# Retention, gated MLP and SoLU on one core: eight half tiles of MLP weights converted one stage earlier, and raw weights loaded two ahead instead of three

## The chip, the core and the metric

One core of one Trainium2 chip runs the whole program. TensorE (PE) multiplies matrices, VectorE (DVE), ScalarE (ACT) and GpSimd (POOL) do the elementwise work, and SyncE (SP) issues every DMA of this kernel. Each engine takes its instructions strictly in the order of its own queue. The metric is the device time in microseconds; the median of three runs before is 684.48 us (682.38 to 685.29).

## The reference

Three layers follow one another over 2304 tokens of 512 features (4 sequences of 576 tokens, 8 heads of 64):

```
scores = scale * q @ k.T                      # per batch and head
x  = (scores * decay_mask) @ v                # decay gamma**(i-j), causal; 2304 x 512
h  = x @ w_in                                 # 512 -> 2048
g  = h * clip(h + 3, 0, 6) / 6
x2 = g @ w_out                                # 2048 -> 512
h2 = x2 @ w2_in                               # 512 -> 1024
solu = h2 * softmax(h2);  ln = layernorm(solu) * g_ln
out = ln @ w2_out                             # 1024 -> 512
```

The MLP weights arrive as 64-bit floats, taken as pairs of 32-bit words. The precision of a product is kept by splitting each operand into two parts (a rounded value and its remainder) and multiplying three of the four combinations, so one logical product is three matmuls.

## The kernel before, in words

**Tiles and stages.** Tokens are cut into five blocks, 0 to 3 of 512 tokens and 4 of 256 (`BLOCKS`). The 2048 hidden features are 16 tiles of 128 ("ff"). The first MLP runs in two parts: the first part takes ff 0 to 5 (`FIRST`) for all five blocks and stores partial sums `x2s` in DRAM; the second part takes ff 6 to 15 (`FB`), adds the stored partial sums and goes on to the second MLP. Attention comes first and is interleaved with block 0 of the first part; then come the end of block 0 beside the h products of block 1 (`mlp_turns`), the x2 products of block 1 (`mlp_x2s(1)`), then blocks 2, 3 and 4.

**One block of the first part** (`mlp`, L250): `mlp_h` (L202) makes, for each ff, 12 matmuls into one PSUM tile; ACT forms `r` from it (L219), DVE forms `gf` (L220), ACT rounds it to `g` (L223) and POOL takes the remainder (L224). `mlp_x2s` (L239) then makes, for each of four quarters `d` of the output, 18 matmuls over the six `g`, and `evac_partial` (L303) lets ACT copy the finished quarter out of PSUM (L305, tile `x2p`) and SP store it (L306). The PSUM tiles of h and of x2 share four buffers ("mm" in two pools of two), so a next h product waits until an earlier quarter has been copied out. The copies use two buffers (`x2e`), so the third copy of a block waits for the store of the first. Each generator yields after three matmuls; in blocks 1 to 3 a yield is three matmuls of 512 columns, 24 yields make the h phase and 24 the x2 phase. Block 4 runs `mlp_by_ff` (L269): h products alone for the first three ff, then h and x2 in turns.

**Conversion of weights** (class `Weights`, L89). Each ff has two halves (w_in and w_out). `load_to(n)` issues DMAs of raw halves (512 KB each, L102) up to number n; the raw tile `wraw` has two buffers (`WRAW`). `step()` loads ahead and converts the next half with `split` (L112): ACT L122, DVE L127, ACT L128, DVE L129, L130 (the last reader of the raw tile), L133, and L136 on DVE or, for every third half, on POOL. `ahead` says up to which half `step` has loads issued before it converts: with three, the load of the half two further on stands in the program before the conversion whose raw buffer it takes over; with two, the load of the next half stands there.

**Order.** The library orders the instructions of each queue when the program is built, from the data they need, the order in which the program traces them and its own planned times; the chip then keeps that order. `keep_in_program_order` fixes an instruction behind the one traced just before it on the same engine. All loads of raw weights (L101 to L103) are fixed in this way on SP, so that each stands behind whatever SP instruction was traced before it.

**Where the conversions stand before.** The 12 halves of ff 0 to 5 are converted during attention and `mlp_turns`. The eight halves of ff 6 to 9 (`FB[:4]`, tag `wb` of pool `pb`) are converted during block 3 of the first part, one at every sixth yield (L590 to L594). The 12 halves of ff 10 to 15 (`FB[4:]`, which take over the buffers of ff 0 to 5) are converted from the middle of block 4 on, through `first_b`, the first block of the second part, which itself begins to run inside the last yields of block 4 (L597 to L607). The 16 halves of the second MLP follow, one every 12 yields.

Of the kernel before, what the change touches and what calls it, by code (L numbers as in the profile page):

```python
# [22 lines left out]
NFF = DFF // 128  # L23
NFF2 = DFF2 // 128
FA = 6
# [12 lines left out]
A_FROM = 4  # L38
TAIL = 2
ACT_W = (1,)  # L40
AHEAD = 3
WRAW = 2
C_AHEAD = 8
EARLY = 3
# [13 lines left out]
def retention_hardswish_solu_kernel(ctx, tc, kt, qt, kn, vt, w1, w2i, w2o, gln, decay, place, out):  # L58
# [10 lines left out]
    def mm_tile(shape, name):  # L69
        turn[0] += 1  # L70
        return ps_mm[(turn[0] // 2) % len(ps_mm)].tile(shape, F32, tag="mm", name=name)
# [17 lines left out]
    class Weights:  # L89


        def __init__(self, halves, pin, ahead=AHEAD):
            self.pin, self.ahead = pin, ahead
            self.todo = list(halves)
            self.raws = []
            self.at = 0
# [47 lines left out]
    def w_half(home, i, name):  # L144

        if home == "w":
            return p0.tile([128, 2, 512], F32R, tag="wi" if i == 0 else "wo", bufs=FA, name=name)
        return pb.tile([128, 2, 512], F32R, tag="wb", bufs=8, name=name)

    def w1_halves(ffs, home, order):  # L150

        for k, i in order:
            ff = ffs[k]
            if (ff, 1 - i) not in w1t and home == "wb":
                for j in range(2):
                    w1t[ff, j] = w_half(home, j, f"w1_{ff}_{j}")

            def tile_of(ff=ff, i=i):
                if home == "w":
                    w1t[ff, i] = w_half(home, i, f"w1_{ff}_{i}")  # L160
                return w1t[ff, i]

            yield w1[ff][:, i * 1024:(i + 1) * 1024], tile_of

    def in_first(n):
        return [(k, i) for i in range(2) for k in range(n)]

    def in_turn(n, ahead):

        return sorted(in_first(n), key=lambda ki: (ki[0] + ahead * ki[1], -ki[1]))  # L170
# [56 lines left out]
    def mlp_x2(acc, ff, d, g, first, last):  # L227
        c = slice(d * 128, (d + 1) * 128)
        for i, (a, b) in enumerate(((0, 0), (1, 0), (0, 1))):
            nc.tensor.matmul(acc, w1t[ff, 1][:, a, c], g[:, b], start=(first and i == 0), stop=(last and i == 2))  # L230

    def mlp_hs(t, ffs, g, slot, keep_x=False):

        for k, ff in enumerate(ffs):
            if keep_x and 0 <= k - 1 < NP:
                tc.keep_in_program_order(nc.sync.dma_start(out=xs[t][:, k - 1], in_=f32(xb[t, k - 1])))
            yield from mlp_h(t, ff, g, slot)

    def mlp_x2s(t, ffs, g, evac):  # L239

        n = BLOCKS[t][1]
        for d in range(NP):
            acc = mm_tile([128, n], f"x2_{t}_{d}")
            for k, ff in enumerate(ffs):
                mlp_x2(acc, ff, d, g[ff], k == 0, k == len(ffs) - 1)
                if k == len(ffs) - 1:
                    evac(t, d, acc)
                yield

    def mlp(t, ffs, slot, evac, keep_x=False):  # L250
        g = {}
        yield from mlp_hs(t, ffs, g, slot, keep_x)
        yield from mlp_x2s(t, ffs, g, evac)

    def mlp_turns(t, g, hs, ffs, evac, ps):

        n = BLOCKS[t][1]
        accs = [ps.tile([128, 2, 512], F32, tag="h2", bufs=2, name=f"acc{t}_{i}") for i in range(2)]
        for k, ff in enumerate(ffs):
            for d in range(NP):  # L260
                mlp_x2(accs[d // 2][:, d % 2], ff, d, g[ff], k == 0, k == len(ffs) - 1)
                if k == len(ffs) - 1:
                    evac(t, d, accs[d // 2][:, d % 2])
            yield k
            for d in range(NP):
                next(hs)
            yield k

    def mlp_by_ff(t, ffs, slot, evac, ps, then=iter(()), n_then=0, ahead=0):  # L269


        n = BLOCKS[t][1]
        share = 512 // n
        accs = [
            ps.tile([128, 2, 512], F32, tag="h2", bufs=2, name=f"acc{t}_{ffs[0]}_{i}").rearrange(
                "p a (b n) -> p (a b) n", n=n
            ) for i in range(2 // share)
        ]
        g, done = {}, []
        last = len(ffs) - 1  # L280
        for k in range(len(ffs) + X2_LAG):
            h = mlp_h(t, ffs[k], g, slot) if k <= last else iter(())
            j = k - X2_LAG
            for d in range(NP):
                next(h, None)
                if 0 <= (k - last - 1) * NP + d + ahead < n_then:
                    next(then, None)
                if j >= 0:

                    acc = accs[d * n // 1024][:, d % (1024 // n)]  # L290
                    mlp_x2(
                        acc, ffs[j], d, g[ffs[j]],
                        j == 0 and d % share == 0, j == last and d % share == share - 1,
                    )
                    if j == last:
                        done.append((d, acc))
                        if (d + 1) * n % 1024 == 0:
                            for item in done:
                                evac(t, *item)
                            done.clear()  # L300
                yield j
# [152 lines left out]
    def attention():  # L454

        for pr in range(NPAIR + 1):
            if pr < NPAIR:
                scores(pr)
                yield pr
                if pr + 2 >= EARLY:  # L460
                    load_pair(pr + 2)
                chunk_states(pr)
                if pr == 0:
                    places()
                prep(pr + 1)
                if pr < NP:
                    widen(pr)
            if pr:
                values(pr - 1)
            yield pr  # L470
            if pr < NPAIR:
                last_scores(pr)
            if pr:
                from_states(pr - 1)
            yield pr
            if pr == 1:
                tc.keep_in_program_order(nc.sync.dma_start(out=gln_sb, in_=gln))
# [21 lines left out]
        )  # L499
    prep(0)  # L500

    FIRST = list(range(FA))
    g_a = lambda ff: (p0, "g", FA)
    g = [{}, {}]
    hs = mlp_hs(0, FIRST, g[0], g_a, True)
    wq = Weights(w1_halves(FIRST, "w", in_first(FA)), True, 2)
    for s, pr in enumerate(attention()):
# [12 lines left out]
    ps_c = tc.alloc_tile_pool(name="ps_c", bufs=1, space=bass.MemoryType.PSUM)  # L520
    hs = mlp_hs(1, FIRST, g[1], g_a, True)
    for i, _ in enumerate(mlp_turns(0, g[0], hs, FIRST, evac_partial, ps_c)):
        if i % 2 == 0:
# [1 line left out]
    wq.step(FA)  # L525
    pa.release()
    pb = tc.alloc_tile_pool(name="pb", bufs=1)
    for _ in mlp_x2s(1, FIRST, g[1], evac_partial):
        pass
    for _ in mlp(2, FIRST, g_a, evac_partial, True):  # L530
        pass
    mlp_3 = mlp(3, FIRST, g_a, evac_partial)


    FB = list(range(FA, NFF))
    g_b = lambda ff: (p0, "g", FA) if ff < 2 * FA else (pb, "g2", NFF - 2 * FA)

    def load_x(t, p):
# [42 lines left out]
    def part_b(t, by_ff=False):  # L581
        load_x2p(t, 0)
        load_x2p(t, 1)
        if by_ff:
            yield from mlp_by_ff(t, FB, lambda ff: (p0, "g", FA), evac_full, ps_c)
        else:
            yield from mlp(t, FB, g_b, evac_full)


    wq = Weights(w1_halves(FB[:4], "wb", in_turn(4, 3)), False)  # L590
    wq.load_to(2)
    for i, _ in enumerate(mlp_3):
        if i % 6 == 0:
            wq.step()  # L594
    first_b = part_b(B_ORDER[0], True)
    wq = None
    for i, j in enumerate(mlp_by_ff(4, list(range(FA)), g_a, evac_partial, ps_c, first_b, X2_LAG * NP)):  # L597
        if j == 0 and wq is None:
            wq = Weights(w1_halves(FB[4:], "w", in_turn(len(FB) - 4, 1)), False)
            wq.load_to(2)  # L600
# [4 lines left out]
    for i, _ in enumerate(first_b):  # L605
        if i % 3 == 0:
            wq.step()  # L607
        j = i - NP * (len(FB) - X2_LAG)
        if 0 <= j < NP:
# [3 lines left out]
    for k, t in enumerate(B_ORDER[1:-1]):  # L613
        after = B_ORDER[k + 2]
        for i, _ in enumerate(part_b(t)):
            if i % STEP_B == STEP_B // 2:
                w2q.step()
            j = i - (4 * len(FB) + 4)
            if after in RELOAD and j >= 0 and j % 4 == 0 and j < 4 * NP:
# [178 lines left out]
```

## Time and profile before

| | |
|---|---|
| median of three runs | 684.48 us |
| the profiled execution, its time | 684.05 us |
| its span in the trace | 682.3 us |
| PE busy | 666.1 us |
| DVE busy | 389.3 us |
| ACT busy | 313.7 us |
| POOL busy | 252.9 us |

The span is what the trace covers, from the first to the last instruction; the execution's own time is 1.75 us longer. A matmul's recorded time overlaps that of the next one, so "busy" of PE is not a measure of its speed; the distance between the starts of matmuls is.

### The profile page before, as it was taken

To read this page: it belongs to the slowest core of one execution; us is meant where nothing else is said; L and a number is where in the kernel's file an instruction comes from. 1 tells how busy PE (TensorE), PEld (TensorE's weight loads), DVE (VectorE), ACT (ScalarE), POOL (GpSimd) and SP (SyncE) were. 2 spreads that over 40 slices of the span, in tenths; PEclk is the share of its full clock that TensorE was granted. 3 is DMA by queue.
4 is the path that set the end of the run, shared out by engine and by line. 5 is a ranking of instruction groups with operands and counts; after the bars stand their busy time and mean duration, and the time that the engine had idled before them with its cause. 6 is when DMAs were issued, how large, how long until landed. Compare 5 with 4: busy or idle time off the path is not lost.

```text
span 682.3 us, 10565 instructions
## 1 busy us (share of the span) xinstructions
PE 666.1 (98%) x3970; PEld 555.5 (81%) x3970; DVE 389.3 (57%) x609; ACT 313.7 (46%) x554; POOL 252.9 (37%) x252
## 2 busy tenths in 40 slices
PE   7899999999998999999999999999999999999998
PEld 4778788888876978887888888889888888888887
DVE  1667667101395859337847735111579776777781
ACT  4767655233353545235235325123346545545363
POOL 3677763223040332326124115334244325232232
PEclk7999999999999999999999999999999999999999
DMA  8789906144425433365962551129345443323332
GB/s 312 255 284 296 311 32 216 47 166 158 144 103 171 139 124 123 124 216 183 332 223 97 215 184 61 28 94 371 127 92 124 89 82 93 78 62 77 78 77 77
DMA packets 74214, 103.46 MB, mean 152 GB/s; under 512 B 42290, under 2 KB 43058, under 8 KB 74164
## 3 DMA queue, kind: packets, MB, share of 16 engines
q1 hardware_dynamic: 74164, 102.80, 47.5%
q8 instruction: 31, 0.51, 0.3%
q14 instruction: 19, 0.16, 0.1%
HBM read 66.08 MB, written 27.26 MB: 137 GB/s over the span
## 4 chain that ended last, share of the span: by engine, by line
PE 81%; DMA 7%; DVE 5%; issue 3%; POOL 2%; ACT 1%; SPq 1%; DVEq 0%; ACTq 0%; POOLq 0%
PE h L209 21%; PE x L230 16%; PE o L699 14%; PE h L634 14%; PE acc L230 9%; DMA rq<-in_qt_dram 3%; PE xp L332 3%; DMA wraw<-in_w_dram 2%; PE s L332 2%; PE u L332 1%; DVE wz L130 1%; POOL g L224 1%; DVE gf L220 1%; DVE wt L127 1%; DMA wraw<-in_w2i_dram 1%
## 5 line engine op out<-in xcount | busy, mean ns | idle before, releaser
L224 POOL TENSOR_TENSOR g<-gf,g 128x512 fp32r<-128x512 f32 (+1 forms) x80 | 100.7, 1261 | 225.8 <-ACT g L223 214.1
L209 PE MATMUL h<-xb,w 128*128 128x512 f32 (+1 forms) x600 | 133.6, 362 | 3.2 <-ACT x2p L305 3.1
L230 PE MATMUL x<-g,w 128*128 128x512 f32 x576 | 133.3, 390 | 1.8 <-POOL g L224 1.0
L230 PEld LDWEIGHTS x<-g,w 128*128 128x128 f32 x576 | 107.7, 188 | 25.8 <-POOL g L224 1.9
L220 DVE SCALAR_TENSOR_TENSOR gf<-r,h 128x512 f32<-128x512 f32 (+1 forms) x80 | 50.3, 630 | 119.0 <-ACT r L219 110.4
L209 PEld LDWEIGHTS h<-xb,w 128*128 128x128 f32 x600 | 100.9, 191 | 19.4 <-ACT x2p L305 4.0
L634 PE MATMUL h<-w2i,x2b 128*128 128x512 f32 x432 | 102.3, 389 | 0.0
L699 PE MATMUL o<-w2o,lt 128*128 128x512 f32 (+1 forms) x456 | 101.2, 378 | 0.0
L699 PEld LDWEIGHTS o<-w2o,lt 128*128 128x128 f32 x456 | 82.5, 188 | 16.0
L634 PEld LDWEIGHTS h<-w2i,x2b 128*128 128x128 f32 x432 | 80.5, 188 | 16.2
L209 PE MATMUL h<-xB,w 128*128 128x512 f32 x360 | 82.4, 389 | 0.0
L200 POOL TENSOR_TENSOR lt<-lT,lt 128x512 fp32r<-128x512 f32 x36 | 45.8, 1293 | 97.4 <-ACT lt L199 97.4
L230 PE MATMUL acc<-g,w 128*128 128x512 f32 (+1 forms) x384 | 80.2, 338 | 1.0 <-POOL g L224 0.7
L223 ACT ACTIVATE g<-gf 128x512 fp32r<-128x512 f32 (+1 forms) x80 | 47.0, 588 | 70.1 <-DVE gf L220 63.6
L209 PEld LDWEIGHTS h<-xB,w 128*128 128x128 f32 x360 | 67.6, 188 | 14.0
L219 ACT ACTIVATE r<-h,half 128x512 f32<-128x512 f32 (+1 forms) x80 | 50.7, 635 | 59.6 <-PE h L209 59.3
L230 PEld LDWEIGHTS acc<-g,w 128*128 128x128 f32 x384 | 63.4, 190 | 11.1 <-POOL g L224 1.1
L127 DVE TENSOR_SCALAR wt<-wz 128x512 int32<-128x512 int32 x48 | 30.2, 630 | 36.5 <-ACT wz L122 35.9
L122 ACT ACTIVATE wz<-wraw 128x512 f32<-128x512 f32 x48 | 32.0, 666 | 27.9 <-DMA wraw<-in_w_dram 11.3
L133 DVE TENSOR_TENSOR wz<-wt,wz 128x512 f32<-128x512 f32 x48 | 41.1, 856 | 1.2
L130 DVE SCALAR_TENSOR_TENSOR wz<-wraw,wz 128x512 f32<-128x512 uint32 x48 | 40.1, 835 | 1.0
L200 POOL TENSOR_TENSOR xb<-xa,xb 128x512 fp32r<-128x512 f32 (+7 forms) x32 | 29.3, 938 | 18.7 <-ACT xb L199 18.7
(78 smaller groups left out, 674.2 us busy)
## 6 DMA issues: line engine op xcount, KB each, us to landing
wraw<-in_w_dram SPq DMA_DIRECT2D x32, 512.0 KB, 3.6
xs<-xb SPq DMA_DIRECT2D x12, 512.0 KB, 5.7
xB<-xs SPq DMA_DIRECT2D x12, 512.0 KB, 5.8
rv<-in_vt_dram SPq DMA_DIRECT2D x16, 288.0 KB, 5.7
x2l<-x2s SPq DMA_DIRECT2D x18, 256.0 KB, 3.7
out_dram<-osb SPq DMA_DIRECT2D x17, 256.0 KB, 2.0
x2s<-x2p SPq DMA_DIRECT2D x16, 256.0 KB, 2.5
wraw<-in_w2i_dram SPq DMA_DIRECT2D x8, 512.0 KB, 5.4
```

The lines of the kernel that those rows point to most:

```text
L130: ve.scalar_tensor_tensor(out=z, in0=raw[:, :, 0].bitcast(U32), scalar=2.0 ** -52, in1=z, op0=ALU.mult, op1=ALU.mult)
L133: ve.tensor_tensor(out=z, in0=f, in1=z, op=ALU.add)
L200: ge.tensor_tensor(out=x[:, 1, c], in0=src, in1=f32(x[:, 0, c]), op=ALU.subtract)
L209: nc.tensor.matmul(hp, w1t[ff, 0][:, a, c], xb[t, p][:, b, :n], start=(p == 0 and i == 0), stop=(p == NP - 1 and i == 2),)
L219: se.activation(out=r, in_=hp, func=ACTF.Relu, scale=1.0 / 6.0, bias=half)
L220: ve.scalar_tensor_tensor(out=gf, in0=r, scalar=1.0, in1=hp, op0=ALU.min, op1=ALU.mult)
L223: se.activation(out=g[ff][:, 0], in_=gf, func=ACTF.Copy)
L224: ge.tensor_tensor(out=g[ff][:, 1], in0=gf, in1=f32(g[ff][:, 0]), op=ALU.subtract)
L230: nc.tensor.matmul(acc, w1t[ff, 1][:, a, c], g[:, b], start=(first and i == 0), stop=(last and i == 2))
L332: keep(nc.tensor.matmul(*args, **kw))
L634: nc.tensor.matmul(h[:, m], x[:, a, c], w[:, b], start=(d == 0 and j == 0), stop=(d == NP - 1 and j == 2),)
L699: nc.tensor.matmul(op, lt[:, a, ff % 4], w[:, b, c0:c0 + n], start=(ff == 0 and j == 0), stop=(ff == NFF2 - 1 and j == 2),)
```

## The change

Two edits. `AHEAD` goes from 3 to 2, which concerns the conversions of ff 6 to 15 and of the second MLP (those of ff 0 to 5 had 2 already). And the queue of conversions for ff 6 to 9 is set up before the x2 products of block 1: one raw half is loaded ahead, and seven conversions are traced at yields 0, 2, 4, 12, 20, 28 and 30 of the chain of block 1's x2 phase (yields 0 to 23) and block 2 (yields 24 to 71). The eighth is traced at yield 8 of block 3. The program's `pb` pool, in which the converted halves live, is opened at the same place as before, just ahead of this chain.

```diff
-AHEAD = 3
+AHEAD = 2
...
-    FIRST = list(range(FA))
+    FIRST, FB = list(range(FA)), list(range(FA, NFF))
...
     wq.step(FA)
     pa.release()
     pb = tc.alloc_tile_pool(name="pb", bufs=1)
-    for _ in mlp_x2s(1, FIRST, g[1], evac_partial):
-        pass
-    for _ in mlp(2, FIRST, g_a, evac_partial, True):
-        pass
+    wq = Weights(w1_halves(FB[:4], "wb", in_turn(4, 3)), False)
+    wq.load_to(1)
+    for i, _ in enumerate(chain(mlp_x2s(1, FIRST, g[1], evac_partial), mlp(2, FIRST, g_a, evac_partial, True))):
+        if i in (0, 2, 4, 12, 20, 28, 30):
+            wq.step()
     mlp_3 = mlp(3, FIRST, g_a, evac_partial)
-    FB = list(range(FA, NFF))
...
-    wq = Weights(w1_halves(FB[:4], "wb", in_turn(4, 3)), False)
-    wq.load_to(2)
     for i, _ in enumerate(mlp_3):
-        if i % 6 == 0:
+        if i == 8:
             wq.step()
```

## Rows read from the trace of the kernel before

**Rows 1.** The page, busy time by engine: us, share of the span, instructions.

```profile
PE 666.1 (98%) x3970; PEld 555.5 (81%) x3970; DVE 389.3 (57%) x609; ACT 313.7 (46%) x554; POOL 252.9 (37%) x252
```

**Rows 2.** Table by stretches: busy us per engine (instructions), granted clock, DMA share, GB/s.

```profile
core 0: us, PE busy (x) PEld busy (x) DVE busy (x) ACT busy (x) POOL busy (x), PEclk, DMA share, GB/s
125.80:144.22 18.42, 18.36 (x82) 14.87 (x81) 0.00 (x0) 3.79 (x8) 2.59 (x2) 1.00 0.16 57
144.22:160.69 16.47, 16.47 (x72) 13.62 (x73) 3.44 (x5) 8.02 (x13) 5.39 (x5) 1.00 0.56 205
160.69:177.01 16.32, 16.32 (x73) 13.52 (x72) 0.69 (x1) 3.01 (x5) 2.32 (x2) 1.00 0.46 164
177.01:193.34 16.33, 16.33 (x74) 13.52 (x73) 10.83 (x15) 8.30 (x14) 4.16 (x3) 1.00 0.40 144
193.34:211.38 18.04, 17.15 (x73) 13.20 (x72) 16.81 (x24) 8.78 (x15) 6.99 (x5) 1.00 0.26 89
211.38:224.77 13.39, 9.99 (x67) 9.29 (x66) 5.19 (x10) 4.42 (x10) 1.47 (x2) 0.87 0.79 234
224.77:229.81 5.04, 5.04 (x44) 5.04 (x43) 4.07 (x8) 3.84 (x8) 1.33 (x2) 1.00 0.17 51
```

**Rows 3.** Timeline of PE: start, us, line, operation, [idle before and its releaser].

```profile
193.34 8.09 PE L230 MATMUL x<-g,w 128*128 128x512 f32 x33
202.32 9.22 PE L230 MATMUL x<-g,w 128*128 128x512 f32 x39 [0.89 <-ACT g L223]
...
215.34 1.69 PE L209 MATMUL h<-xb,w 128*128 128x256 f32 x12 [0.92 <-ACT x2p L305]
219.21 2.11 PE L209 MATMUL h<-xb,w 128*128 128x256 f32 x10 [2.18 <-ACT x2p L305]
```

**Rows 4.** Timeline of ACT around the start of block 4.

```profile
210.43 1.07 ACT L305 ACTIVATE x2p<-x 128x512 f32<-128x512 f32 x2
214.69 0.60 ACT L305 ACTIVATE x2p<-x 128x512 f32<-128x512 f32 x1 [3.19 <-DMA x2s<-x2p]
216.88 0.66 ACT L122 ACTIVATE wz<-wraw 128x512 f32<-128x512 f32 x1 [1.60 <-DMA wraw<-in_w_dram]
...
218.57 0.58 ACT L305 ACTIVATE x2p<-x 128x512 f32<-128x512 f32 x1
```

**Rows 5.** Timeline of ACT and of SP: block 0's last copy, the first loads.

```profile
139.04 0.60 ACT L305 ACTIVATE x2p<-acc 128x512 f32<-128x512 f32 x1 [0.32 <-PE acc L230]
178.31 0.88 SPq L102 DMA_DIRECT2D wraw<-in_w_dram  x2
```

**Rows 6.** Tile wraw from 177 to 275 us: landing times; then its last reader L130.

```profile
L130 DVE SCALAR_TENSOR_TENSOR wz<-wraw,wz x20: 677/692/1681, 184.0 to 274.5; 128x512 f32<-128x512 uint32 x20
...
DMA to landing us min/median/max: 2.8/3.5/6.1
```

**Rows 7.** The conversions' instructions alone (tile wz), by stretches: DVE, ACT, POOL busy.

```profile
182.40:200.92 18.52, 15.51 (x18) 3.29 (x5) 1.29 (x1) 1.00 0.24 88
...
216.80:222.00 5.20, 2.93 (x5) 0.66 (x1) 0.00 (x0) 0.78 0.81 244
```

**Rows 8.** Timeline of DVE and POOL in block 3.

```profile
183.56 0.43 DVE L129 TENSOR_SCALAR wz<-wt 128x512 int32<-128x512 int32 x1
...
187.75 1.35 POOL L224 TENSOR_TENSOR g<-gf,g 128x512 fp32r<-128x512 f32 x1 [2.62 <-ACT g L223]
187.86 1.53 DVE L129 TENSOR_SCALAR wz<-wt 128x512 int32<-128x512 int32 x1
...
200.92 0.68 DVE L220 SCALAR_TENSOR_TENSOR gf<-r,h 128x512 f32<-128x512 f32 x1
```

**Rows 9.** Timeline of SP in block 4 and after; then PE's first h of ff 15.

```profile
247.54 3.05 SPq L306 DMA_DIRECT2D x2s<-x2p  x4
250.69 17.78 SPq L102 DMA_DIRECT2D wraw<-in_w_dram  x6
...
276.08 0.84 PE L209 MATMUL h<-xb,w 128*128 128x512 f32 x3
```

**Rows 10.** The page, DMA issues: count, KB each, median us to landing.

```profile
wraw<-in_w2i_dram SPq DMA_DIRECT2D x8, 512.0 KB, 5.4
```

## The prediction

> **What bounds the kernel now.** I read the page's busy times first. TensorE is busy in 98% of the span and no other engine in more than 57% [rows 1], so time can come only from where TensorE runs slower than it can. The next view is therefore the table by stretches, cut at the phases of blocks 1 to 4. In an undisturbed phase (block 2's x2, block 3's h) 72 matmuls of 512 columns take 16.32 and 16.33 us, 0.2267 us each; in block 4's steady part 42 matmuls of 256 columns take 5.04 us, 0.12 us each [rows 2]. Measured with these, two neighbouring phases fall short. Block 3's x2 phase takes 18.04 us, 1.72 too long. The stretch after it holds 66 matmuls of 256 columns, worth 7.92 us, and takes 13.39, 5.47 too long; its granted clock is 0.87 where the phases around it have 1.00, so part of the loss is matmuls at the lower of the two levels, 1.2 GHz, after TensorE had stood idle [rows 2]. Together 7.19 us, the only loss here that belongs to the eight conversions.
>
> The timelines then say why. In block 3 TensorE runs 33 x2 matmuls and waits for the last g [rows 3]; that g's DVE step starts at 200.92 [rows 8], 7.6 us after its h product ended at 193.34, because conversions stand ahead of it in DVE's queue: DVE is busy 16.81 of 18.04 us there [rows 2]. At block 4's start TensorE waits twice for ACT's copy of x2 out of PSUM [rows 3]. These copies come late because ACT's queue holds conversions too: the third copy waits for the first one's store, and the fourth stands behind a conversion that waits for its raw half to land [rows 4]. In contrast DVE does nothing in the 18.42 us of block 1's x2 phase and 0.69 us in block 2's [rows 2].
>
> **The change, part by part.** *Removed:* seven of eight conversions leave block 3, the eighth stays at its yield 8 with its raw half long loaded. Seven are enough to take both losses away: DVE then has some 3 us of extra work in block 3, less than block 2's idle 15.6 us. Gain 7.19 us, bounds 5.47 (only the second loss goes) and 7.19. What is next in line in that place is block 4's own chain from h to g, which costs nothing at 0.12 us per matmul in 224.77 to 229.81.
>
> *Moved:* when can the new conversions begin? The first load is fixed on SP behind the store of block 0's last quarter, whose copy starts at 139.04 and takes 0.60 [rows 5]. The same pattern before was a load at 178.31, directly behind block 2's last store. So the load goes out near 140.1, lands 3.5 us later (bounds 2.8 and 6.1) [rows 6], at 143.6, and DVE starts on it after ACT's 0.66, at 144.3. The idle DVE of block 1's x2 phase is thus hardly used, though three steps are traced there: the work falls into block 2's h phase. That costs in two places.
>
> (a) Block 2's start. At 144.22 the four copies of block 1 are due, and the next h products need their buffers, as at block 4's start. ACT may sit on a conversion whose half has not landed, and SP on a load that waits for a raw buffer, with stores queued behind it. Upper bound 5.47 us, what this cost at block 4. Lower bound -0.15, the excess of 16.47 over 16.32 that block 2's h phase has already. A 512-column h product takes 12 x 0.2267 = 2.72 us against 1.44 for 256 columns, so buffers are wanted half as fast; I take 0.5, near the row of the same place.
>
> (b) Block 2's x2 phase. Conversions stand ahead of its last g in DVE's queue as in block 3. Lower bound 0, as block 2 has now; upper bound 12.3, worked out under the slower rival. Nearest is block 3's own 1.72 us, with four conversions ahead of the last g. Here up to seven are traced ahead of it, but with 16 us to do them, not 10, and the order of the matmuls is laid out when the program is built: in block 3 it already put 33 matmuls before the first that needed the last g. I take 1.7.
>
> (c) Two ahead, not three, for ff 10 to 15. Before, six raw halves were issued ahead of block 4's four stores and six after them, at 250.69, spread over 17.78 us [rows 9], so 3.5 us apart; the last reader of the last half starts at 274.5 [rows 6]. Now the load of the sixth half stands behind those stores too, so every half is one pace later. The w_in of ff 15, the last but one, then takes the old time of the last: its L130 at 274.5 and three DVE steps of 0.7 after it, ready at 276.6, while its first product starts at 276.08 [rows 9] and needs the remainder half a microsecond later. That is no slack. Lower bound 0, upper bound 2.6 (a landing of 6.1, not 3.5); I take 0.3, since all 3.5 us come from median landings. ACT's r and g queue behind a conversion that waits so, and TensorE behind them.
>
> (d) The second MLP's halves: 12 yields of 0.68 are 8.2 us between steps, more than a landing of 5.4 [rows 10] less the overlap of two buffers: (5.4 + 3.9) / 2 = 4.7 us a half. Nothing. If that cover went, ACT would wait for each half. The instructions converted are the same in number, as are the loads; the SP queue gets no new entry. The small stalls later (near 248 and 323 us) I leave as they are.
>
> Sum against the profiled execution: 684.05 - 7.19 + 0.5 + 1.7 + 0.3 = 679.36. The median of the runs is 684.48, 0.43 above that execution, so I forecast 679.8.
>
> **A rule weighed.** DVE's L129 takes 0.43 us alone and 1.53 us while POOL works on a g [rows 8]; a conversion's DVE steps take 2.93 us with POOL idle, and 15.51 us for four in block 3, 3.9 each [rows 7]. The Trainium skill, GPSIMD Engine Reference, section "8. Key points", says that GpSimd shares its SBUF interfaces with VectorE and that DVE instructions with two SBUF inputs or in a two-port mode contend with it; the trace agrees. It speaks against the change: by it the conversions that fall beside block 2's POOL work are the dear ones, which is the second rival.
>
> **The rivals.** *1. Nothing is given back.* If the loads go out earlier or the planned order of matmuls leaves room for the late g (four PSUM buffers hold 60 matmuls, 13.6 us, that need only the first five g), then 684.05 - 7.19 + 0.43 = 677.3. For it: DVE's idle 18.42 us. Against: the place of the first load on SP.
>
> *2. DVE beside POOL.* POOL has 2.59 us of work up to 144.22 and 5.39 in block 2's h phase [rows 2]. Three conversions at 2.93 and four at 3.9, with five gf of 0.68, are 27.8 us from 144.3: the last gf starts at 172.1, and its matmul 1.4 us later (in block 3 from 200.92 to 202.32), at 173.5. After 33 matmuls TensorE gets there at 160.69 + 7.5 = 168.2, so it stands 5.3 us: 684.05 - 7.19 + 0.5 + 0.3 + 5.3 + 0.43 = 683.4. The rule named above is this one. Against: the order laid out may put more than 33 first.
>
> *3. The PSUM wait moves.* Block 2's start costs block 4's 5.47 instead of 0.5: 684.8. For it: loads, stores and copies meet at 144. Against: buffers wanted half as fast.
>
> *4. Slower: the last g of block 2 behind all seven conversions.* If all run at 3.9 us, the last gf starts at 144.3 + 27.3 + 3.4 = 175.0, its matmul at 176.4. If TensorE's order asks for that g in the first quarter, after 15 matmuls at 164.1, it stands 12.3 us: 684.05 - 7.19 + 0.5 + 0.3 + 12.3 + 0.43 = 690.4. It decides from a stand of 6.4 us on, where the gain is gone, and counts as slower from 9.8 us. Against: with 33 matmuls first, as in block 3, the same lateness costs 8.2 us, 686.3, no measurable change.
>
> **How the numbers follow.** Forecast 0.48 (own range 677.5 to 682.5), rival 1 0.12, rival 2 0.12, rival 3 0.12, rival 4 0.16. The range 676.0 to 685.5 leaves out most of rival 4 and little else. Half a percent, 3.4 us, is about what can be told from no change: faster means below 681.1. Four fifths of the forecast and rival 1 with a small part of rival 2 lie there, 0.55; rivals 2 and 3, the rest of the forecast and the mild end of rival 4 are the same, 0.32; slower 0.13.
>
> **What would show it.** Block 3's x2 phase at 16.3 us, and no idle before block 4's h products, with a clock of 1.00 there, show the removal right. The first moved load near 140 and DVE busy from 144 on show the move. TensorE's phases of block 2, at most 17 us for h and 18 for x2, show (a) and (b); the wait for w_in of ff 15 shows (c). The prediction is wrong if block 4's start still waits, or if block 2 loses more than 4 us.

## The result and the profile after

The changed kernel takes 676.87 us (median of four runs, 675.46 to 678.01) against 684.36 before (a fourth run joined the three of the table of before): a ratio of 0.9891, interval 0.9866 to 0.9916. The forecast was 679.8 with a range of 676.0 to 685.5. The profiled execution takes 678.01 us with a span of 676.3, that is 6.04 and 6.0 less than before.

The table by stretches of the changed kernel, cut at the same phases as [rows 2] (block 1's x2; block 2's h and x2; block 3's h and x2; block 4's start of 66 matmuls; its steady part):

```profile
124.97:143.55 18.58, 18.52 (x83) 15.02 (x81) 13.04 (x19) 8.59 (x16) 4.08 (x3) 1.00 0.36 113
143.55:160.02 16.47, 16.47 (x72) 13.62 (x73) 9.51 (x13) 8.87 (x15) 4.23 (x3) 1.00 0.59 197
160.02:179.28 19.26, 17.23 (x73) 13.23 (x72) 10.12 (x13) 6.55 (x11) 6.29 (x5) 1.00 0.69 255
179.28:195.60 16.32, 16.32 (x73) 13.51 (x72) 3.44 (x5) 7.21 (x11) 5.39 (x5) 1.00 0.05 17
195.60:211.92 16.32, 16.32 (x73) 13.51 (x72) 0.69 (x1) 3.01 (x5) 2.32 (x2) 1.00 0.25 81
211.92:219.84 7.92, 7.92 (x68) 7.92 (x67) 3.06 (x6) 5.14 (x11) 2.20 (x3) 1.00 0.53 167
219.84:224.88 5.04, 5.04 (x45) 5.04 (x44) 5.04 (x11) 2.78 (x7) 0.97 (x2) 1.00 0.36 122
```

Line by line against [rows 2]: block 3's x2 phase fell from 18.04 to 16.32, block 4's start from 13.39 to 7.92 at a clock of 1.00, and block 2's x2 phase rose from 16.32 to 19.26. DVE's 0.00 in block 1's x2 phase became 13.04. The timeline of PE (answering [rows 3]) shows where block 2 waits:

```profile
160.02 2.20 PE L230 MATMUL x<-g,w 128*128 128x512 f32 x9
163.45 1.66 PE L230 MATMUL x<-g,w 128*128 128x512 f32 x6 [1.23 <-ACT g L223]
165.28 4.59 PE L230 MATMUL x<-g,w 128*128 128x512 f32 x19 [0.17 <-POOL g L224]
170.51 8.94 PE L230 MATMUL x<-g,w 128*128 128x512 f32 x38 [0.64 <-ACT g L223]
179.28 16.48 PE L209 MATMUL h<-xb,w 128*128 128x512 f32 x72
```

It waits three times: after 9 matmuls for the rounded part of the fourth g, after 6 more for that g's remainder, and after 34 in all for the last g, where block 3 before waited only once, after 33, for the last. Which g it was shows in DVE's timeline, by the step that ACT rounds to g next: the fourth and the last in the changed kernel's block 2, then the same two in block 3 before:

```profile
162.06 0.67 DVE L220 SCALAR_TENSOR_TENSOR gf<-r,h 128x512 f32<-128x512 f32 x1
169.11 0.68 DVE L220 SCALAR_TENSOR_TENSOR gf<-r,h 128x512 f32<-128x512 f32 x1
```

```profile
192.88 0.68 DVE L220 SCALAR_TENSOR_TENSOR gf<-r,h 128x512 f32<-128x512 f32 x1
200.92 0.68 DVE L220 SCALAR_TENSOR_TENSOR gf<-r,h 128x512 f32<-128x512 f32 x1
```

The timeline of SP shows when the raw halves were loaded (the load at 110.18 is the twelfth, the last of ff 0 to 5):

```profile
110.18 0.33 SPq L102 DMA_DIRECT2D wraw<-in_w_dram  x1
110.56 2.15 SPq L236 DMA_DIRECT2D xs<-xb  x3
116.77 11.81 SPq L102 DMA_DIRECT2D wraw<-in_w_dram  x3
128.68 0.38 SPq L306 DMA_DIRECT2D x2s<-x2p  x1
130.70 0.33 SPq L102 DMA_DIRECT2D wraw<-in_w_dram  x1
135.61 8.71 SPq L306 DMA_DIRECT2D x2s<-x2p  x5
144.43 0.40 SPq L102 DMA_DIRECT2D wraw<-in_w_dram  x1
```

Three halves are loaded before the first store of block 0, the first of them at 116.77, and none waits for its last. Four conversions are done in block 1's x2 phase; the fifth load stands behind block 1's second store, at 144.43, and the last four conversions fall beside block 2's g. The eighth is among them: it is traced at yield 8 of block 3, but its L122 starts at 163.88, and in block 3 DVE has nothing but the g (3.44 and 0.69 us).

**The account**, profile to profile: 0.67 us had gone before block 2's h (144.22 to 143.55; the head, below), +2.94 in block 2's x2, -1.73 in block 3, -5.47 at block 4's start, and -1.07 after it: 6.00 in all. Of the last term 1.01 is the stall near 248 us of before, 6.45 us for 24 matmuls, which now take 5.44 (24 x 0.2267). Before it was this wait:

```profile
248.52 0.50 PE L230 MATMUL acc<-g,w 128*128 128x512 f32 x1 [0.71 <-POOL g L224]
```

**The median moved more than the profiles.** Two of the four runs take 678.0 us, the profiled one among them; two take 675.5 and 675.8 and have no trace. The traces of other executions show one place where they differ, the stretch from 10 to 20 us: first the profiled execution, then a repetition of the same kernel (after_third), then experiment 4:

```profile
10.00:20.00 10.00, 10.00 (x142) 7.92 (x142) 2.81 (x10) 6.03 (x16) 4.84 (x12) 0.76 1.05 396
```

```profile
10.00:20.00 10.00, 9.90 (x181) 8.64 (x180) 4.08 (x15) 7.64 (x20) 6.96 (x14) 1.00 1.05 395
```

```profile
10.00:20.00 10.00, 10.00 (x116) 7.75 (x116) 2.89 (x9) 5.13 (x14) 3.77 (x10) 1.00 1.03 377
```

TensorE got through 142 matmuls in the first and 181 in the second, and block 2's h began at 143.55 and 141.77. The granted clock (0.76 and 1.00) goes with that here, but not in experiment 4, where it is recorded as 1.00 and TensorE does only 116; so the recorded clock alone does not explain a run's time. In experiment 1, too, a run with 1.000 over the whole span takes 678.44. The stretch lies in attention, which the change does not touch. The profile of before has 138 matmuls there, so the profiles' 6.0 compares like with like; the first 20 us are the likely reason why the medians differ by 7.5.

### The profile page after: what moved, and what is told of

It is laid out like the page before. It is cut to its first block, busy times and chain, and to the rows that moved or that the text cites. A ratio compares the mean times of both kernels' runs of the same rounds, so it can differ in the third digit from the quotient of the medians.

```text
span 676.3 us, 10560 instructions
## 1 busy us (share of the span) xinstructions
PE 664.0 (98%) x3970; PEld 554.4 (82%) x3970; DVE 389.9 (58%) x609; ACT 314.3 (46%) x554; POOL 253.4 (37%) x252
## 4 chain that ended last, share of the span: by engine, by line
PE 85%; DMA 6%; DVE 4%; issue 2%; POOL 1%; ACT 1%; SPq 1%; DVEq 0%; ACTq 0%; POOLq 0%
PE h L209 22%; PE x L230 17%; PE o L697 15%; PE h L632 14%; PE acc L230 10%; PE xp L332 3%; DMA rq<-in_qt_dram 3%; PE s L332 2%; PE u L332 1%; DMA wraw<-in_w2i_dram 1%; DVE gf L220 1%; DMA wraw<-in_w_dram 1%; DVE wt L127 1%; DMA raw<-in_kn_dram 1%; DVE wz L130 1%
## 5 line engine op out<-in xcount | busy, mean ns | idle before, releaser
L209 PE MATMUL h<-xb,w 128*128 128x512 f32 (+1 forms) x600 | 131.9, 359 | 0.1
L127 DVE TENSOR_SCALAR wt<-wz 128x512 int32<-128x512 int32 x48 | 30.3, 632 | 47.2 <-ACT wz L122 47.0
L122 ACT ACTIVATE wz<-wraw 128x512 f32<-128x512 f32 x48 | 31.8, 665 | 48.6 <-DMA wraw<-in_w_dram 16.7
L130 DVE SCALAR_TENSOR_TENSOR wz<-wraw,wz 128x512 f32<-128x512 uint32 x48 | 42.0, 875 | 1.0
L133 DVE TENSOR_TENSOR wz<-wt,wz 128x512 f32<-128x512 f32 x48 | 38.1, 793 | 1.3
L665 ACT ACTIVATE lh<-ln 128x1024 uint16<-128x1024 uint16 x18 | 19.0, 1056 | 36.9 <-DVE ln L658 36.8
```

What stands on the lines that cost most here:

```text
L130: ve.scalar_tensor_tensor(out=z, in0=raw[:, :, 0].bitcast(U32), scalar=2.0 ** -52, in1=z, op0=ALU.mult, op1=ALU.mult)
L133: ve.tensor_tensor(out=z, in0=f, in1=z, op=ALU.add)
L209: nc.tensor.matmul(hp, w1t[ff, 0][:, a, c], xb[t, p][:, b, :n], start=(p == 0 and i == 0), stop=(p == NP - 1 and i == 2),)
```

## The experiments

Theory A is the prediction's: the gain is the two stalls of blocks 3 and 4, less what block 2 gives back. B says that the gain comes from loads two ahead, C that what leaves one place of block 2 comes back at another, D that both edits mend the same stall at block 4's start. Experiments 1 to 4 ran on one chip, 5 to 8 on a second, 9 to 11 on a third; each ratio is to runs of the kernel before on the same chip.

**1. The change once more** (no edit).

> The changed kernel once more, beside the others. Theory A (the gain is the two stalls of blocks 3 and 4, less what block 2 gives back) and theory B (the gain comes from loads two ahead) expect the same here: 676 to 678 us, block 2's x2 phase near 19.3 us, block 3's near 16.3, the 66 matmuls at block 4's start 7.9.

676.98 us, ratio 0.9890 (0.9868 to 0.9913). As before within the noise; block 2's x2 phase takes 19.10, block 3's 16.32.

**2. The move alone.**

```diff
-AHEAD = 2
+AHEAD = 3
```

> The moved conversions with loads three ahead. A: blocks 3 and 4 as in the changed kernel (16.3 and 7.9 us), so 5.5 to 7.5 us below before, 677 to 679; the fifth load stands earlier on SP than in the changed kernel, so block 2's x2 phase may lose less than 2.9 us. B: most of the gain gone, 682 to 684.

677.52 us, 0.9891 (0.9875 to 0.9908): the whole gain without the other edit. Block 3's x2 takes 16.32 us, and block 2's 18.28, not 19.1. The fifth load stands one place earlier and its half is converted in block 1's x2 phase (L122 at 139.96), so three conversions are left beside block 2's g; they still cost 1.96.

**3. Loads two ahead alone** (the kernel before, with `AHEAD = 2`).

> The conversions where they were, loads two ahead. A: block 3's x2 phase still near 18.0 us and block 4's start near 13.4; only the 1.0 us stall near 248 us may go, 683 to 684.5. B: 677 to 679, with block 4's start near 8 us.

679.29 us, 0.9929 (0.9911 to 0.9947). A's expectation failed: this edit alone makes the kernel 4.9 us faster than the runs before on its chip (684.17), though less than the move. The table shows block 3's x2 phase and then 80 matmuls of block 4, worth 9.6 us:

```profile
191.42:209.37 17.95, 17.08 (x74) 13.20 (x72) 14.37 (x20) 8.30 (x15) 6.98 (x5) 1.00 0.40 127
209.37:219.53 10.16, 9.89 (x81) 9.61 (x80) 7.12 (x14) 5.84 (x13) 1.70 (x2) 1.00 0.76 243
```

Block 3's loss stays; of block 4's 5.47 us, 0.64 is left (by the starts in PE's timeline the first 78 matmuls take 10.00 us where 9.36 are due). ACT's timeline says why: the first two copies now stand ahead of the seventh conversion, and the third follows them, where in [rows 4] they came at 210.43 behind it.

```profile
203.96 1.07 ACT L305 ACTIVATE x2p<-x 128x512 f32<-128x512 f32 x2
208.00 0.60 ACT L305 ACTIVATE x2p<-x 128x512 f32<-128x512 f32 x1 [2.96 <-DMA x2s<-x2p]
209.28 0.66 ACT L122 ACTIVATE wz<-wraw 128x512 f32<-128x512 f32 x1 [0.68 <-DMA wraw<-in_w_dram]
```

With two ahead the seventh load is traced after block 3's first store and stands behind it on SP (205.03 after 204.57, where before all seven go out ahead of that store), and that conversion is laid out later. And term (c) of the prediction shows up here:

```profile
271.00 0.50 PE L209 MATMUL h<-xb,w 128*128 128x512 f32 x1 [1.29 <-DVE w L136]
```

The first product of ff 15 waits for its weight's remainder. From the end of the stall near 248 to the last x2 products (244.03 to 275.91) it takes 31.88 us, against 29.69 in experiment 1 (245.72 to 275.41): 2.2 us.

**4. All eight conversions early.**

```diff
-        if i in (0, 2, 4, 12, 20, 28, 30):
-            wq.step()
+        if i < 4:
+            wq.step(2)
...
-    for i, _ in enumerate(mlp_3):
-        if i == 8:
-            wq.step()
+    for _ in mlp_3:
+        pass
```

> All eight conversions traced at the first four yields of block 1's x2 phase, two at each, none in block 3. A with its cause (DVE's queue ahead of block 2's last g): all done near 152 us, before most of block 2's g, so block 2's x2 phase is back at 16.3 to 16.8 us and the time 2.5 to 3 us below the changed kernel, 673.5 to 675. Rival C (ACT's and SP's queues hold up the copies of block 1, so the wait moves to the start of block 2): block 2's h phase 18 us or more, and no gain over the changed kernel.

679.76 us, 0.9937 (0.9913 to 0.9962), slower than the changed kernel. Both theories are half right. PE, then ACT:

```profile
148.39 16.62 PE L209 MATMUL h<-xb,w 128*128 128x512 f32 x72 [3.45 <-ACT x2p L305]
164.85 16.48 PE L230 MATMUL x<-g,w 128*128 128x512 f32 x72
181.17 16.48 PE L209 MATMUL h<-xb,w 128*128 128x512 f32 x72
```

```profile
144.32 0.67 ACT L122 ACTIVATE wz<-wraw 128x512 f32<-128x512 f32 x1 [1.91 <-DMA wraw<-in_w_dram]
144.89 0.58 ACT L305 ACTIVATE x2p<-acc 128x512 f32<-128x512 f32 x1
145.48 0.63 ACT L128 ACTIVATE w<-wt 128x512 fp32r<-128x512 f32 x1
147.18 0.67 ACT L122 ACTIVATE wz<-wraw 128x512 f32<-128x512 f32 x1 [1.07 <-DVE wz L130]
147.76 1.07 ACT L305 ACTIVATE x2p<-x 128x512 f32<-128x512 f32 x2
```

Block 2's x2 phase is back at 16.32 (164.85 to 181.17), so conversions ahead of its g were the cause of the 2.94. But block 1's copies, due by 144.9, when TensorE runs out of work, now stand behind the sixth and seventh conversion, which wait for a load and a buffer, and TensorE waits 3.45 us: the prediction's rival 3, met here and not in the change. By the phases this trade costs some 0.5 us (3.45 less 2.94); the other 2 us between the medians are not explained by them. The profiled execution also has the slowest first 20 us of all the profiles.

**5. Five early, three in block 2's x2 phase.** Yields 0, 1, 2, 3 and 48, 54, 60, 66, nothing in block 3; the fifth half's load goes out with the fourth step, so its conversion runs early too (L122 at 135.88). The sixth was laid out at the end of block 2's h (154.52).

```diff
-        if i in (0, 2, 4, 12, 20, 28, 30):
+        if i in (0, 1, 2, 3, 48, 54, 60, 66):
```

> Loads two ahead; conversions traced at yields 0 to 3 (block 1's x2 phase) and 48, 54, 60, 66 (block 2's x2 phase), none in block 3. In DVE's queue five conversions stand ahead of block 2's first gf and less than one between there and its last; in ACT's queue five stand ahead of block 1's copies, against seven with all early. Theory A (block 2's x2 phase loses by conversions ahead of the last g, its start by conversions ahead of the copies): x2 phase 16.3 to 16.8 us, no wait over 1 us before block 2's h, 2 to 3 us below the changed kernel, 673.5 to 675. Rival C (what leaves one place of block 2 comes back at the other): 676 to 678.

675.17 us, 0.9867 (0.9839 to 0.9894). Block 2's h and x2 phases:

```profile
140.97:157.42 16.45, 16.45 (x72) 13.64 (x73) 4.92 (x8) 8.91 (x15) 5.16 (x4) 1.00 0.69 236
157.42:173.74 16.32, 16.32 (x73) 13.53 (x72) 3.48 (x7) 5.16 (x9) 4.23 (x3) 1.00 0.66 230
```

Neither place loses, as A had it; the median lies 0.2 us above A's range, below C's.

**6. One more ahead of the copies** (yields 0 to 4 and 48, 56, 64).

> The same with yields 0 to 4 and 48, 56, 64: a sixth conversion stands ahead of block 1's copies in ACT's queue. A: x2 phase of block 2 at 16.3, and a wait of 1 to 2 us before its h, between four_four and all early: 675 to 676.5. C: as four_four.

675.01 us, 0.9857 (0.983 to 0.9884). The wait before block 2's h is there, between none and 3.45; its price in the median is below the spread of the runs.

```profile
143.01 16.64 PE L209 MATMUL h<-xb,w 128*128 128x512 f32 x72 [1.48 <-ACT x2p L305]
```

**7. Loads two ahead for the first eight halves only** (the kernel before).

```diff
-    wq = Weights(w1_halves(FB[:4], "wb", in_turn(4, 3)), False)
+    wq = Weights(w1_halves(FB[:4], "wb", in_turn(4, 3)), False, 2)
```

> The kernel before, with loads two ahead for the first eight halves only and three for the other 28. If the two edits overlap at block 4's start (theory D: loads two ahead alone let ACT copy before it converts there), this keeps ahead_only's gain there and drops its cost near 271 us: 2 us below ahead_only, 676.5 to 678, with no wait for DVE's L136 near 271. If the gain of ahead_only lies in the later loads instead (theory B), 683 to 685.

678.84 us, 0.9910 (0.9884 to 0.9935). Block 4's start is mended whole: its first 52 matmuls run without a wait, and 66 take 7.92 us.

```profile
211.13 6.40 PE L209 MATMUL h<-xb,w 128*128 128x256 f32 x52
217.37 0.40 PE L230 MATMUL acc<-g,w 128*128 128x256 f32 x2
```

The wait near 271 is gone (245.83 to 275.53 is 29.7 us), as D had it; the loads of the first eight halves carry the whole gain of that edit. Measured against its own chip's 685.41 the gain is 6.6 us; the median is 0.8 us above the expected range.

**8. POOL out of block 2.**

```diff
-        ge.tensor_tensor(out=g[ff][:, 1], in0=gf, in1=f32(g[ff][:, 0]), op=ALU.subtract)
+        if t == 2 and ff < FA:
+            se.activation(out=g[ff][:, 1], in_=gf, func=ACTF.Copy)
+        else:
+            ge.tensor_tensor(out=g[ff][:, 1], in0=gf, in1=f32(g[ff][:, 0]), op=ALU.subtract)
```

> The changed kernel, with the remainder of block 2's six g in the first part replaced by a plain copy on ACT, so that part of the result is wrong and POOL has only one conversion's last step there. If POOL beside DVE makes block 2's late g: DVE's L127, L129 and L130 back at 0.43, 0.43 and 0.69 us each, block 2's x2 phase at 16.3 to 17.3 and the time 2 to 3 us below the changed kernel, 674 to 675. If the number of DVE's steps makes it: x2 phase still 18.5 to 19.3, 676.5 to 678.

This kernel leaves out the remainder of block 2's g: a plain copy on ACT stands in its place. It takes 675.8 us, 0.9866 (0.9841 to 0.9891), 0.8 above the expected range, and its interval overlaps the change's, so it is the trace that tells. The conversions' instructions in block 2 (columns as in [rows 7]), in the changed kernel and here:

```profile
143.55:170.50 26.95, 16.27 (x19) 2.67 (x4) 1.48 (x1) 1.00 0.75 264
```

```profile
143.70:170.00 26.30, 11.17 (x19) 2.67 (x4) 1.35 (x1) 1.00 0.84 286
```

```profile
160.17 16.48 PE L233 MATMUL x<-g,w 128*128 128x512 f32 x72
```

The same 19 DVE steps take 5.1 us less when POOL has but one step there, and block 2's x2 phase is 16.32 (160.17 to 176.49). So with POOL out, four conversions in that place cost it nothing. The copy on ACT also ends earlier than POOL's remainder did, but the last g's DVE step itself comes 5.6 us earlier in the phase (163.69 after 160.17, against 169.11 after 160.02).

**9 to 11. On one chip: the change, experiment 5 again, and its like with loads three ahead** (`AHEAD = 3`, yields 0, 1, 2 and 48, 52, 56, 60, 64).

> The changed kernel on the same chip as four_four, for a direct comparison: 676 to 678 us.

> Five conversions in block 1's x2 phase and three in block 2's. By the traces 2.9 us below the changed kernel, from block 2's x2 phase alone: 673.5 to 675 where that one shows 676 to 678.

> The same five and three with loads three ahead everywhere (traced at yields 0, 1, 2 and 48, 52, 56, 60, 64). If loads two ahead matter only through the order at block 4's start (theory D), nothing is left for them to do here: equal to four_four within 1 us. If they matter in the later conversions (theory B), 1 us or more above it, with new waits after 210 us.

676.48 us (0.9877, 0.9858 to 0.9896), 674.88 (0.9853, 0.983 to 0.9876) and 675.64 (0.9857, 0.9833 to 0.9881). Experiment 5's kernel has the lowest median seen (experiment 6's cannot be told from it), 1.6 us below the change in the median; the intervals overlap, and it is the traces that part the two, by block 2's x2 phase (16.3 to 16.4 in the kernels of experiments 5 and 11, 19.2 in the change). With nothing left to mend at block 4's start, two or three ahead makes no difference that can be told.

## Why the prediction was right, and where it was not

**The removal** was right in both size and place: 7.19 us forecast, 7.20 measured (1.73 and 5.47), the clock at block 4's start back at 1.00.

**What it missed about the removal.** It took the second stall as the work of the conversions' number. Experiments 3 and 7 leave all eight conversions traced where they were and mend 4.83 and all of its 5.47 us. What differs in ACT's timeline there is an order: ACT copies block 3's first quarters before it converts the seventh half, not after it. No run swaps these two alone. Either edit mends that. So the edits overlap: alone they bring 6.7 and 4.9 us, together 7.2.

**The failing step is "Moved".** It said that the first load is fixed on SP behind block 0's last store and goes out near 140.1. It went out at 116.77, ahead of the first of these stores (128.68). The stores are traced before it, but they were not what it was fixed behind. What was is not shown: between stores and load the program closes one tile pool and opens another, which may be it; no run tests that. So four conversions, not none, ran in the idle DVE of block 1's x2 phase, and four, not up to seven, beside block 2's g. Rival 1's condition, loads that go out earlier, was met, and its 677.3 lies nearer to the median than the forecast; but it has nothing given back, and block 2 gave back 2.94.

**(a)** was 0.5 and came out at 0: the phase takes 16.47 as before. Experiments 4 and 6 show the wait is real, 3.45 and 1.48 us, with seven and six conversions ahead of the copies; the change has four.

**(b)** was 1.7 and measured 2.94 (the phase took 19.26 us, where the prediction allowed 18), and its path was wrong in part. It looks at the last g alone. That was asked for after 34 matmuls, as in block 3 after 33, and cost 0.9 us; so rival 4's condition, the last g wanted in the first quarter, was not met. The other 1.9 went on the fourth g, which the prediction had not counted (both worked out from the starts in PE's timeline, at 0.2267 us per matmul). TensorE wanted that g after 9 matmuls, 2.04 us into the phase, and just then, at 162.06, DVE's step for it started; in block 3 before, the same step had started 0.46 us ahead of the phase (192.88 and 193.34). Rival 2's cause, DVE beside POOL, is what makes the g late (experiment 8); its sum of 5.3 was too high with three conversions too many.

**(c)** was 0.3 and came out at 0. Taken alone the edit does cost 2.2 us, inside the bounds of 0 to 2.6 (experiment 3); in the changed kernel ff 15 does not wait. What spares it there was not tried.

**Left uncounted**: the stall near 248, which I left as it was, lost its 1.0 us. It is gone in every kernel with moved conversions and down to single waits of 0.2 to 0.5 us in the two with the old place; which instruction's order made it was not tried.

In sum the prediction had 679.36 for the profile, which took 678.01, and that it came so near is partly luck. Beside a removal that was right, (a) and (c) were 0.8 too dear and (b) 1.2 too cheap, with conversions in another place than it had them; the 248 stall and what followed it (1.07) and the head (0.67) it did not count. What lies between that and the median of 676.87 is, as far as the traces tell, the first 20 us.

## What to carry to other kernels

A stall at one engine can be the order of two instructions in another engine's queue; before paying for a move of work, look whether the waiting copy merely stands behind a conversion that could stand behind it. Idle time of an engine is worth only as much as its inputs arrive in it: here DVE had 18 us free, and which stores the loads stand behind on SP decided how much of it was used. Work moved to DVE should land where POOL is idle too: the same 19 DVE steps cost 11.2 us or 16.3.

## What the runs showed of the hardware

The size of DVE's stretch beside POOL: the 19 steps of experiment 8 went from 16.27 to 11.17 us when POOL's work was taken out of the place, including the one-input L127 and L129, which took 1.51 and 1.40 us beside POOL's steps (at 159.19 and 160.74) and 0.43 alone. The Trainium skill, GPSIMD Engine Reference, section "8. Key points", says that GpSimd shares its SBUF interfaces with VectorE and contends with DVE instructions that have two SBUF inputs or run in a two-port mode. These runs agree; in which mode L127 and L129 ran, no trace here shows.

TensorE's pace in the first 20 us differs between executions of one kernel: the same group of 16 matmuls in attention took 2.08 us in the profiled execution of the change (at 11.62) and 1.16 in its repetition (at 10.47), with a granted clock of 0.76 and 1.00 from 10 to 20 us, and all that follows came 1.8 us later in the first. Experiment 4's profile has the slow 2.08 too (at 12.38), with a clock recorded as 1.00. There the pace of the matmuls tells more than the recorded clock.
